# Due times of all engines' steps taken from one table, and the last output block copied and sent in two halves

## The chip, the cores and the metric

The kernel runs on one core of one Trainium2 chip. The metric is the device time of one execution in microseconds; of several executions the median counts. The core's engines each work through a queue of their own, in order: TensorE (PE: matmuls, with weight loads PEld beside them), VectorE (DVE), ScalarE (ACT), GpSimd (POOL) and SyncE (SP, which here only issues DMAs). An instruction that waits holds up all that stands behind it in its queue.

## The reference

Attention with a window of 128 positions and a bias by distance, then a feed-forward layer with a squared ReLU, all in float32:

```python
scores = scale * np.matmul(q, k.transpose(0, 1, 3, 2)) + bias          # 8 batches, 8 heads, 576 positions, 64 wide
scores = np.where((rel >= 0) & (rel < 128), scores, -1e9)
attn = softmax(scores)
x = (attn @ v).transpose(0, 2, 1, 3).reshape(4608, 512)
h = np.maximum(x @ w_in, 0.0)                                           # 512 x 2048
out = h * h @ w_out                                                     # 2048 x 512
```

## The kernel before

The 4608 tokens are cut into nine **chunks** `c` of 512. Attention goes by **couples** `q` (chunk and pair of heads, four to a chunk), each of two **segments** `k = 2q + s` of 256 positions. The float32 matmuls of the feed-forward layer are made of three products of rounded high and low parts (`hh`, `hl`; `w` likewise). The first layer of chunks 0 and 1 is plain (`gemm1`, L224); from chunk 2 on it is done by a scheme of seven products of half size (`M1` to `M7`, L319, in the PSUM tiles `chain` and `rest`), whose weight sums are computed once, during chunk 1, by DVE, ACT and POOL (`weight_sums`), written to DRAM (`ws`) and streamed back for each use (`flow`, L288). A step `n` of this part handles two of the 16 blocks of a hidden layer. The second layer's blocks (`("g", f, m)`, L376) fill the PSUM tiles `acc`; when a chunk is full, `give` copies each of the four blocks to an `o` tile (L382, even blocks on DVE, odd ones on ACT) and `send` writes it out (L386). There are four `o` tiles; some `weight_sums` and pieces of attention use them as well.

Once in two steps `n`, a **visit** `q` (class `Visit`) puts attention work on PE: `one` and `two` multiply the values with the masked weights of couple q-1 (L719), and between them `scores` makes the scores of couple q (L732). What lies between the scores of a couple and the next visit is a long chain over the other engines, for each segment:

- `base` (ACT, L613 and L620) and `fold` (DVE, L632 and L636) move the scores to an SBUF tile `t`;
- `t` (DVE, L400, four) adds the bias and takes the maximum, `e` (ACT, L407, four) the exponentials, `sum` (DVE, L414 and L415) the reciprocal;
- `norm` (POOL, L419) multiplies, `square` (DVE, L471) transposes in squares of 32;
- `write` (SP, L475, four DMAs to the DRAM tile `way`) and `read` (SP, L480) finish the transpose;
- `before` and `same` (POOL, L484) mask the two halves, after which the next visit's `one` can run.

Beside this chain run the drains of the seven products (`s1`, `R`, `s2`, `C21` on ACT; `C11`, `C22`, `C12` on DVE, L324, of which M3 needs C11 and M4 needs C22), the squares `sq`, `high` and `hl` of the hidden layer (L346, L351, L353), and the pieces `x` of the last couple's result (L669 and L684 to L704).

The order of all queues is set in Python when the program is built. `Plan.add` takes each step's engine, its planned length, what it follows, and a **due** time; `Plan.run` repeatedly takes the engine that can start first, and of that engine's steps that can start at about that time the one that is due first. Planned lengths and dues decide the order only: on the chip each engine waits for what it needs. PE's steps are each tied to the PE step before, so their order doesn't depend on dues. Steps with the same due and time are taken in the order of a Python set, which can differ from build to build: rows of an order below are those of one build each. `start` plans the beginning with dues of its own, `middle` all from the second chunk's first layer on.

Of the kernel before, what the change touches and what calls it, by code (L numbers as in the profile page):

```python
# [24 lines left out]
NCH = B * S // 512  # L25
# [6 lines left out]
WAIT = 0.1  # L32
HAND = {"SP": 2.0, "PE": 0.25}
PORT = ('t', 'c', 'h1')
# [29 lines left out]
class Kern:  # L64
# [315 lines left out]
    def give(self, c, m):  # L380
        o = self.out[c, m] = self.op.tile([128, 512], F32, name="o")
        (self.nc.scalar.copy if m % 2 else self.nc.vector.tensor_copy)(o, self.full.pop((c, m)))  # L382

    def send(self, c, m):
        out = self.outd[m * 128 : m * 128 + 128, 512 * c : 512 * c + 512]
        (self.nc.scalar if c == NCH - 1 and m == 3 else self.nc.sync).dma_start(out, self.out.pop((c, m)))  # L386
# [428 lines left out]
class Plan:  # L815


    def __init__(self, wait=WAIT, port=PORT):
        self.steps, self.count, self.wait, self.port = {}, {}, wait, port
# [12 lines left out]
    def run(self):  # L832
# [7 lines left out]
        while near:  # L840
# [16 lines left out]
            same = [r for r in ready if self.steps[r[2]][0] == on and r[0] <= first[0] + max(0.1, self.wait * span)]  # L857
# [132 lines left out]
ACT, DVE, POOL = "Activation", "DVE", "Pool"  # L990
SOFT = dict(M1=0.72, g=0.7, first=2.79, one=0.85, scores=0.75, two=0.65)
# [9 lines left out]
def middle(K, waiting):  # L1001
    P = Plan(0.7, ("t", "ws"))
# [15 lines left out]
    def second(count):  # L1018
        for _ in range(count):
# [6 lines left out]
            if e == NF - 1:  # L1026
                P.add(("give", c, m), ACT if m % 2 else DVE, 0.6, (("g", f, m),), t + 1.5, do(K.give, c, m), "o")
                P.add(("send", c, m), "SP", 0.8, (("give", c, m),), t + 8, do(K.send, c, m), None, "o", 1)

    def chain(q, s, V):  # L1030
        G, k = waiting[q].both[s], 2 * q + s
        n = lambda a, *m: (a, k, *m)
        for m in range(4):
            P.add(n("t", m), DVE, 0.22, (n("t", m - 1) if m else n("fold"),), V + 1.8 + 1.4 * s, do(G.top, m))
            P.add(n("e", m), ACT, 0.4, (n("t", m),) + ((n("e", m - 1),) if m else ()), V + 2 + 1.5 * s, do(G.exp, m))
        P.add(n("sum"), DVE, 0.42, (n("e", 3),), V + 2.4 + 1.4 * s, G.sums)
        P.add(n("norm"), POOL, 1.15, (n("sum"),), V + 2.4 + 1.4 * s, G.norm)
        turned(q, s, V + 2.5 + 1.4 * s, (n("norm"),))
# [11 lines left out]
    def visit(q):  # L1050
# [8 lines left out]
        if new and q + 1 < 4 * NCH:  # L1059
            for a, us in (("qk", 1.4), ("v", 0.9)):  # L1060
                fn = K.load_v if a == "v" else lambda c, p: (K.load_qk(c, p, 0), K.load_qk(c, p, 1))
                P.add((a, q + 1), "SP", us, ((a, q),) if (a, q) in P.steps else (), base + 12 if a == "qk" else base + 14, do(fn, *divmod(q + 1, 4)), a)
# [9 lines left out]
        if G.p < 2:  # L1072
# [3 lines left out]
            dues, reads, room = [16, 16.5, 16, 16.5, 18, 19], (0, 1, 2, 3), {0: ("o", None)}  # L1076
# [203 lines left out]
```

## Time and profile before

| what | value |
|---|---|
| median of 3 runs | 917.92 us (917.68 to 919.81) |
| the profiled execution | 919.04 us |
| its span, first to last instruction | 917.3 us |
| granted TensorE clock | 1.00 throughout |
| instructions | 23301 |
| moved by DMA | 212.96 MB, 232 GB/s on average |

The page gives for each engine the time that it was busy and its share of the span; a row of a timeline has the start (us from the span's start), the length, the engine, the line, the operation with its tiles (out<-in) and a count where equal instructions follow each other; idle time of the engine just before, and what ended it, stands in brackets. SPq and ACTq are rows of DMAs being issued by SP and ACT. In a row of a group, the numbers behind the bar are busy time, the mean of one in ns, and idle time before it. In a row of DMA issues they are the KB of each and the median time from issue to landing. An engine's row in the list of waits has the total, the count and the longest wait.

### The profile page before, as it was taken

How to read it: one execution, taken by the hardware profiler on the slowest of the kernel's cores; microseconds unless marked ns; L12 is line 12 of the kernel's file. 1: busy time of each engine (PE TensorE's matmuls, PEld its weight loads, DVE VectorE, ACT ScalarE, POOL GpSimd, SP SyncE). 2: the span in 40 equal slices, each digit the busy share in tenths (PEclk: the TensorE clock that was granted, in tenths of full speed). 3: DMA queues.
4: the chain of work that ended last, by engine and by line, in shares of the span. 5: the costliest groups of instructions: out<-in, count | busy, mean ns of one | idle time of the engine just before them, and what ended most of it. 6: DMA issues, size and time to landing. Idle time of an engine off the chain costs nothing.

```text
span 917.3 us, 23301 instructions
## 1 busy us (share of the span) xinstructions
PE 905.9 (99%) x8500; PEld 803.1 (88%) x8500; DVE 584.1 (64%) x1595; ACT 466.8 (51%) x1321; POOL 275.8 (30%) x339
## 2 busy tenths in 40 slices
PE   9999999999999999999999999999999999999998
PEld 5688888888889999999999999999999989989997
DVE  6999862776766666565756666667666565554333
ACT  7898663566555545444544544445444454433222
POOL 4213324665732223223322332233223232230000
PEclk9999999999999999999999999999999999999999
DMA  9985328668788888777877778777877776666541
GB/s 343 404 309 170 87 61 265 192 204 282 255 274 278 303 276 276 245 231 228 267 248 246 228 234 278 233 239 234 277 230 238 229 251 197 199 208 216 175 127 46
DMA packets 137425, 212.96 MB, mean 232 GB/s; under 512 B 15200, under 2 KB 49120, under 8 KB 137312
## 3 DMA queue, kind: packets, MB, share of 16 engines
q1 hardware_dynamic: 136880, 210.82, 71.5%
q8 instruction: 68, 1.11, 0.5%
q10 hardware_dynamic: 432, 0.66, 0.3%
q14 instruction: 45, 0.37, 0.1%
HBM read 170.52 MB, written 40.89 MB: 230 GB/s over the span
## 4 chain that ended last, share of the span: by engine, by line
PE 87%; DMA 7%; DVE 2%; ACT 1%; issue 1%; SPq 1%; POOL 1%; POOLq 0%; DVEq 0%; ACTq 0%
PE acc L376 41%; PE chain L319 16%; PE rest L319 12%; PE g L224 8%; PE s L719 4%; PE g L732 2%; DMA raw<-in_dram 2%; DMA qk<-in_dram 1%; PE s L732 1%; DMA ws<-both 1%; DMA flow<-ws 1%; PE at L496 1%; DMA way<-pp 1%; DMA wide<-in_dram 1%; POOL pp L484 1%
## 5 line engine op out<-in xcount | busy, mean ns | idle before, releaser
L376 PE MATMUL acc<-hh,w 128*128 128x512 f32 x1152 | 405.1, 397 | 0.0
L376 PEld LDWEIGHTS acc<-hh,w 128*128 128x128 f32 x1152 | 225.6, 196 | 38.5 <-issue 5.3
L376 PE MATMUL acc<-hl,w 128*128 128x512 f32 x576 | 226.3, 393 | 0.0
L484 POOL TENSOR_SCALAR_AFFINE_SELECT pp<-pp 128x512 f32<-128x512 f32 x128 | 101.8, 796 | 204.5 <-DMA pp<-way 73.9
L324 DVE TENSOR_TENSOR four<-four,rest 128x256 f32<-128x256 f32 x112 | 47.2, 422 | 178.1 <-PE rest L319 176.8
L419 POOL TENSOR_TENSOR t<-t,nm 128x512 f32<-128x512 f32 x64 | 73.3, 1147 | 280.5 <-DVE nm L415 241.1
L319 PEld LDWEIGHTS rest<-xu,flow 128*128 128x128 f32 x1008 | 146.3, 196 | 12.7 <-DVE four L324 0.5
L319 PE MATMUL chain<-tees,flow 128*128 128x256 f32 x1008 | 148.3, 283 | 0.3 <-POOL tees L669 0.3
L319 PE MATMUL rest<-xu,flow 128*128 128x256 f32 x1008 | 148.4, 284 | 0.0
L319 PEld LDWEIGHTS chain<-tees,flow 128*128 128x128 f32 x1008 | 133.1, 197 | 0.9 <-POOL tees L669 0.5
L339 ACT COPY four<-chain 128x256 f32<-128x256 f32 x56 | 20.9, 373 | 221.2 <-PE chain L319 221.2
L376 PEld LDWEIGHTS acc<-hl,w 128*128 128x128 f32 x576 | 112.6, 195 | 12.7 <-DVE hl L353 0.2
L407 ACT ACTIVATE t<-t,nm 128x128 f32<-128x128 f32 x256 | 101.1, 399 | 26.5 <-DVE nm L400 26.3
L224 PE MATMUL g<-xu,w 128*128 128x512 f32 x384 | 95.2, 397 | 0.7 <-ACT r L233 0.7
L224 PEld LDWEIGHTS g<-xu,w 128*128 128x128 f32 x384 | 76.3, 209 | 13.8 <-ACT r L233 1.2
L400 DVE CUSTOM_DVE_ANT_0 t<-t,cst 128x128 f32<-128x128 f32 x256 | 68.5, 314 | 1.2
L632 DVE COPY_PREDICATED t<-cst,s 64x256 f32<-64x256 int32 x100 | 44.6, 446 | 32.6 <-PE s L719 22.4
L471 DVE STREAM_TRANSPOSE pp<-t 128x512 f32<-128x512 f32 x64 | 45.4, 710 | 18.8 <-POOL t L419 18.0
L719 PE MATMUL s<-pp,v 64*64 64x128 f32 (+1 forms) x1792 | 52.7, 248 | 3.3 <-POOL pp L484 2.9
L319 PEld LDWEIGHTS chain<-xu,flow 128*128 128x128 f32 x336 | 48.7, 196 | 4.2
L319 PE MATMUL chain<-xu,flow 128*128 128x256 f32 x336 | 49.4, 284 | 0.0
L407 ACT ACTIVATION_READ_ACCUMULATOR t<-t,nm 128x1 f32 x256 | 49.0, 191 | 0.0
(104 smaller groups left out, 1129.6 us busy)
## 6 DMA issues: line engine op xcount, KB each, us to landing
flow<-ws SPq DMA_DIRECT2D x392, 256.0 KB, 4.0
raw<-in_dram SPq DMA_DIRECT2D x32, 512.0 KB, 8.7
way<-pp SPq DMA_DIRECT2D x256, 64.0 KB, 2.0
pp<-way SPq DMA_DIRECT2D x64, 256.0 KB, 3.6
qk<-in_dram SPq DMA_DIRECT2D x32, 320.0 KB, 4.5
v<-in_dram SPq DMA_DIRECT2D x32, 320.0 KB, 3.5
qk<-in_dram SPq DMA_DIRECT2D x38, 256.0 KB, 4.8
out_dram<-o SPq DMA_DIRECT2D x35, 256.0 KB, 3.1
```

The source lines that it names most:

```text
L224: nc.tensor.matmul(g, w, xs[cc][:, part], start=i == 0, stop=i == 11)
L319: self.nc.tensor.matmul(to, w, x, start=start and k == 0, stop=k == 5, skip_group_check=True)
L324: add = lambda to, x: nc.vector.tensor_tensor(to, to, x, op=ALU.add)
L376: self.nc.tensor.matmul(self.acc[m], w, h, start=(f == 0 and i == 0), stop=(f == NF - 1 and i == 2))
L400: self.nc.vector.tensor_tensor_reduce(self.t[:, m], self.t[:, m], self.K.nrel(2 * self.p + m // 2), -0.125, BIG, ALU.add, ALU.min, self.nm ...
L407: return self.nc.scalar.activation(self.t[:, m], self.t[:, m], AF.Exp, bias=nm[:, 4 + m : 5 + m], scale=-1.0, accum_out=nm[:, m : m + 1],)
L419: self.nc.gpsimd.tensor_tensor(*(x.rearrange("p (j i) c -> p j i c", j=2) for x in (self.t, self.t)), self.rec.unsqueeze(3).to_broadcast([ ...
L471: nc.vector.transpose(squares.rearrange("p b m c -> p m b c"), self.t.rearrange("p m (b c) -> p m b c", c=32))
L484: nc.gpsimd.affine_select(to, self.own, pattern=[[-32 * sign, 4], [0, 4], [-sign, 32]], compare_op=op, fill=0.0, base=0, channel_multiplie ...
L632: nc.vector.copy_predicated(d, mask.unsqueeze(1).to_broadcast([64, 2, 2, 64]), e)
L719: yield self.nc.tensor.matmul(to, w, x, start=first and n < 2, stop=not first, skip_group_check=True)
L732: made = self.nc.tensor.matmul(to, w, x, start=not extra, stop=True, skip_group_check=True)
```

## The change

`LAG` and `DUE` are new tables that take the place of the dues that stood in the code, for every family of steps in `middle`: the chain of attention, the drains' followers, output copies and sends, loads, weight sums, streams. `V` is the planned end of a visit, `t` and `now` the planned end of a PE step. Some dues now lie far before or after the time at which a step can run, so that they act as ranks. `Plan` gets a flag `mixed`: where the first step that can start is one that shares a port in the plan (POOL's, and DVE's `t` and `ws`), the choice is among such steps of both engines. The window in which a later step may be taken first goes from 0.7 to 0.4 of a step's length. The last output block (chunk 8, block 3) is copied half by ACT and half by DVE, and sent in two halves by ACT and SP.

```diff
     def give(self, c, m):
         o = self.out[c, m] = self.op.tile([128, 512], F32, name="o")
+        if (c, m) == (NCH - 1, 3):
+            x = self.full.pop((c, m))
+            self.nc.scalar.copy(o[:, 0:256], x[:, 0:256])
+            self.nc.vector.tensor_copy(o[:, 256:512], x[:, 256:512])
+            return
         (self.nc.scalar.copy if m % 2 else self.nc.vector.tensor_copy)(o, self.full.pop((c, m)))
 
     def send(self, c, m):
         out = self.outd[m * 128 : m * 128 + 128, 512 * c : 512 * c + 512]
-        (self.nc.scalar if c == NCH - 1 and m == 3 else self.nc.sync).dma_start(out, self.out.pop((c, m)))
+        o = self.out.pop((c, m))
+        if (c, m) == (NCH - 1, 3):
+            self.nc.scalar.dma_start(out[:, 0:256], o[:, 0:256])
+            self.nc.sync.dma_start(out[:, 256:512], o[:, 256:512])
+            return
+        self.nc.sync.dma_start(out, o)
...
-            same = [r for r in ready if self.steps[r[2]][0] == on and r[0] <= first[0] + max(0.1, self.wait * span)]
+            alike = lambda name: self.steps[name][0] == on or self.mixed and self.shares(first[2]) and self.shares(name)
+            same = [r for r in ready if alike(r[2]) and r[0] <= first[0] + max(0.1, self.wait * span)]
...
+DUE = {
+    "wait": (0.4, 1), "give": (41.7, 32.5, 45.4, 45.4), "send": (43.2,), "load": (4.4, 9.8), "fill": (45.2, -26.7),
...
-    P = Plan(0.7, ("t", "ws"))
+    P = Plan(DUE["wait"][0], ("t", "ws"), DUE["wait"][1])
...
-            P.add(n("t", m), DVE, 0.22, (n("t", m - 1) if m else n("fold"),), V + 1.8 + 1.4 * s, do(G.top, m))
+            P.add(n("t", m), DVE, 0.22, (n("t", m - 1) if m else n("fold"),), V + DUE["t"][s], do(G.top, m))
```

What this does to the queues shows in three places. With the lines added to `give` and `send`, numbers behind them are ten higher in the changed kernel (L386 is L396, L400 is L410, L471 is L481, L475 is L485, L480 is L490).

**SP ahead of visit 13.** The rows run from the first write (`way<-pp`) of couple 12 to its second read (`pp<-way`); `flow` are streamed weight sums, `out_dram` the sends of chunk 1, `ws` writes of weight sums. Before:

```order
L475 DMA way<-pp 32x4x128 x4
L288 DMA flow_6_1686<-ws_109 128x512
L288 DMA flow_0_1673<-ws_110 128x512
L480 DMA pp<-way 128x512
L288 DMA flow_1_1674<-ws_110 128x512
L386 DMA out_dram<-o 128x512 x2
L475 DMA way<-pp 32x4x128 x4
L386 DMA out_dram<-o 128x512 x2
L480 DMA pp<-way 128x512
```

Now, from the stream ahead of the writes on:

```order
L288 DMA flow_4_1677<-ws_110 128x512
L485 DMA way<-pp 32x4x128 x8
L490 DMA pp<-way 128x512
L284 DMA ws_114<-both_2391 128x512
L490 DMA pp<-way 128x512
L284 DMA ws_114<-both_2391 128x512 x3
```

Both segments' writes now stand together, ahead of both reads, with one write of weight sums between the reads; the four sends have moved behind two more steps of streams.

**DVE ahead of visit 33**, in step n = 56. L400 with its maximum is a `t` of couple 32's second segment, the L324 rows are C11, C22 and C12, L414 and L415 a `sum`, L382 an output copy of chunk 6, L471 (L481) the `square`, `ISA` the instructions of L400 (L410). Before, from a `t` to the second square:

```order
L400 ISA nm 128x1
L324 TENSOR_TENSOR four_1687<-four_1687,rest 128x256
L324 TENSOR_TENSOR four_1688<-four_1688,chain 128x256
L400 ISA t,nm<-t,cst 128x128
L400 ISA nm 128x1
L353 TENSOR_TENSOR hl<-spare,hh 128x512
L324 TENSOR_TENSOR four_1687<-four_1687,rest 128x256
L414 TENSOR_SCALAR nm<-nm 128x3x2
L415 RECIPROCAL nm<-nm 128x2x2
L346 SCALAR_TENSOR_TENSOR r<-four_1687 128x512
L382 COPY o<-acc 128x512
L471 STREAM_TRANSPOSE pp<-t 128x4x4x32
```

Now, from the end of the last `t` on:

```order
L410 ISA nm 128x1
L424 TENSOR_SCALAR nm<-nm 128x3x2
L425 RECIPROCAL nm<-nm 128x2x2
L679 TENSOR_TENSOR o<-o,s 128x256
L679 TENSOR_TENSOR xu<-s,xu 128x256
L424 TENSOR_SCALAR nm<-nm 128x3x2
L425 RECIPROCAL nm<-nm 128x2x2
L481 STREAM_TRANSPOSE pp<-t 128x4x4x32
L324 TENSOR_TENSOR four_1687<-four_1687,rest 128x256
L481 STREAM_TRANSPOSE pp<-t 128x4x4x32
L324 TENSOR_TENSOR four_1688<-four_1688,chain 128x256
L324 TENSOR_TENSOR four_1687<-four_1687,rest 128x256
```

All eight `t` and both sums have moved ahead of C11, and both squares ahead of C12. How C11, C22 and the squares stand to each other differs by visit: in the visits 17 to 19, 21 to 23, 25 to 27 and 29 to 31 both squares stand directly ahead of C11, where the second one stood behind C22 before. Ahead of visit 13 it is C11, C22 and then both squares. In most visits the `hl` of the step before (L353, second) has moved ahead of the folds.

**SP at the start of `middle`**, around the sends of chunk 0. `qk` and `v` are loads of keys, queries and values of later couples; `ws_108<-o` is the copy of an `o` tile that `weight_sums` filled. Before:

```order
L475 DMA way<-pp 32x4x128 x8
L480 DMA pp<-way 128x512 x2
L258 DMA ws_108<-o 128x512
L386 DMA out_dram<-o 128x512 x2
L258 DMA ws_108<-w_250 128x512 x2
L170 DMA qk<-in_dram 128x640
```

Now:

```order
L490 DMA pp<-way 128x512
L170 DMA qk<-in_dram 128x640
L170 DMA qk<-in_dram 128x512
L490 DMA pp<-way 128x512
L175 DMA v<-in_dram 128x640
L170 DMA qk<-in_dram 128x640
L170 DMA qk<-in_dram 128x512
L396 DMA out_dram<-o 128x512
L258 DMA ws_109<-w_292 128x512
L258 DMA ws_108<-o 128x512
L258 DMA ws_108<-w_250 128x512 x2
```

Two couples' keys and one's values have moved ahead of the first send and of that copy. The output copies of blocks 2 and 3 of chunk 0 are the fifth and sixth users of the four `o` tiles; in the changed program the first of them waits for a DMA out of a tile, the other for POOL and a DMA.

More of the change, by code (lines that the diff above doesn't have):

```diff
@@ L990 @@
 ACT, DVE, POOL = "Activation", "DVE", "Pool"
+LAG = {"a0": 6.5, "r0": 3, "s2": 1.5, "h0": 1.5, "l0": 0.5, "w0": 0.5}
+DUE = {
+    "wait": (0.4, 1), "give": (41.7, 32.5, 45.4, 45.4), "send": (43.2,), "load": (4.4, 9.8), "fill": (45.2, -26.7),
+    "base": (-0.7, -16.2), "fold": (-0.3, -21.4), "t": (-71.3, -85.5), "e": (-38, 3.5), "sum": (-31.2, -14.7),
+    "norm": (-33.7, -13.5), "square": (-5.5, -3.6), "first": (-800, -11.2, 10.8, -31.4),
+    "ws": (-14.6, 6.7, -2.7, 31.8, 26.2, 25.3, 29.3, 73.4), "flow": (35.1, 33.2), "sq": (-12.7, 34.4),
+    "high": (-11.2, -14.3), "hl": (-14.3, -2.2), "early": (40.9, 16.3, 33.8, 53.7, 7.9, 22.8),
+    "third": (74.8, 68.8, 53.8, 52, 54.4, 50.8, 73.6, 80.8, 46.8, 54.8, 59.5, 61.6),
+    "last": (-1.9, -17, -18.3, 18, -19.2, -31.5, -13.2, 11, -9.1, 0.3, -27.1, -17.4),
+}
 SOFT = dict(M1=0.72, g=0.7, first=2.79, one=0.85, scores=0.75, two=0.65)
@@ L1033, in chain @@
         for m in range(4):
-            P.add(n("t", m), DVE, 0.22, (n("t", m - 1) if m else n("fold"),), V + 1.8 + 1.4 * s, do(G.top, m))
[L1035 to L1038, printed above, removed]
+            P.add(n("t", m), DVE, 0.22, (n("t", m - 1) if m else n("fold"),), V + DUE["t"][s], do(G.top, m))
+            P.add(n("e", m), ACT, 0.4, (n("t", m),) + ((n("e", m - 1),) if m else ()), V + DUE["e"][s], do(G.exp, m))
+        P.add(n("sum"), DVE, 0.42, (n("e", 3),), V + DUE["sum"][s], G.sums)
+        P.add(n("norm"), POOL, 1.15, (n("sum"),), V + DUE["norm"][s], G.norm)
+        turned(q, s, V + DUE["square"][s], (n("norm"),))
     def turned(q, s, d, after):
@@ L1075, in visit @@
             )
[L1076 removed]
+            dues, reads, room = DUE["early"], (0, 1, 2, 3), {0: ("o", None)}
         else:
@@ L1093, in visit @@
                 prior = prior if prior[0] in P.steps else ()
[L1094 removed]
+                P.add(n("fill", s), POOL if late else "free", 0.4 * late, prior, base + DUE["fill"][s], do(new.fill, s), "t")
                 P.add(
[L1096 removed]
+                    n("base", s), ACT, 1.2 if late else 0.58, (n("scores"), n("fill", s)) + behind("base"), V + DUE["base"][s],
                     do(new.base, s, False), None, ("one", "two") if s else None,
                 )
[L1099 removed]
+                P.add(n("fold", s), DVE, 1.15 if late else 0.9, (n("base", s),) + behind("fold"), V + DUE["fold"][s], do(new.fold, s))
             chain(q, 0, V)
@@ L1115, in middle @@
                 (name, n), engine, us, ((("first", n),), (("relu", n),), (("sq", n),), (("high", n),))[i],
-                t + (-800, 2.5, 3.2, 4)[i], step, (("r", "hh"), None, None, None)[i], (("one", "two"), None, None, "r")[i],
+                t + DUE["first"][i], step, (("r", "hh"), None, None, None)[i], (("one", "two"), None, None, "r")[i],
             )
```

30 lines of the change are left out of this document (13 added, 17 removed).

## The prediction

> **What bounds the kernel now.** I read the page first: which engine fills the span.
>
> ```profile
> PE 905.9 (99%) x8500; PEld 803.1 (88%) x8500; DVE 584.1 (64%) x1595; ACT 466.8 (51%) x1321; POOL 275.8 (30%) x339
> ```
>
> TensorE is busy for 905.9 of 917.3 us, and the change leaves its instructions and their order in `middle` as they are (each PE step is tied to the one before it). So only time in which PE stands still can be won, and a new order can only add such time elsewhere. Second view: who PE waits for (us in total, times, longest).
>
> ```profile
> PE s L719 <- POOL pp L484: 2.9, 2, 2.1
> ```
>
> It sits where a "visit" begins: the first L719 matmuls read tiles that POOL's affine selects (L484) have just masked. Third view: the timeline of PE, rows of L719 that begin a visit (start, length).
>
> ```profile
> 232.59 0.90 PE L719 MATMUL s<-pp,v 64*64 64x64 f32 x32
> 258.48 0.33 PE L719 MATMUL s<-pp,v 64*64 64x64 f32 x2
> ...
> 285.00 0.90 PE L719 MATMUL s<-pp,v 64*64 64x64 f32 x32
> 309.13 0.90 PE L719 MATMUL s<-pp,v 64*64 64x64 f32 x32
> ...
> 695.64 0.79 PE L719 MATMUL s<-pp,v 64*64 64x64 f32 x28
> 719.85 0.90 PE L719 MATMUL s<-pp,v 64*64 64x64 f32 x32
> 744.41 0.33 PE L719 MATMUL s<-pp,v 64*64 64x64 f32 x2
> 769.80 0.90 PE L719 MATMUL s<-pp,v 64*64 64x64 f32 x32
> ```
>
> Between two visits PE always does the same work, so distances tell what is lost better than idle rows do. Undisturbed it is 24.13 (285.00 to 309.13). From visit 12 (232.59) to 13 it is 25.89, from 13 to 14 it is 26.52: 1.76 + 2.39 = **4.15 us lost**. Late in the kernel the pace is 24.21 (695.64 to 719.85); then 24.56 and 25.39: 0.35 + 1.18 = **1.53 us lost** around visit 33. Together 5.68 us can be won in the middle, and something at the tail. No other visit is off pace.
>
> **Visit 13 (terms: -4.15, and what is left).** The chain ahead of it, from the timelines of POOL, DVE and SP:
>
> ```profile
> 241.30 0.90 DVE L632 COPY_PREDICATED t<-cst,s 64x256 f32<-64x256 int32 x2
> 245.21 1.14 DVE L400 CUSTOM_DVE_ANT_0 t<-t,cst 128x128 f32<-128x128 f32 x1
> 247.83 1.05 POOL L419 TENSOR_TENSOR t<-t,nm 128x512 f32<-128x512 f32 x1 [1.62 <-DVE nm L415]
> 249.34 0.70 DVE L471 STREAM_TRANSPOSE pp<-t 128x512 f32<-128x512 f32 x1
> 250.56 1.88 SPq L475 DMA_DIRECT2D way<-pp  x4
> 252.48 0.94 SPq L386 DMA_DIRECT2D out_dram<-o  x2
> 255.51 0.33 SPq L480 DMA_DIRECT2D pp<-way  x1
> 258.98 1.84 POOL L484 TENSOR_SCALAR_AFFINE_SELECT pp<-pp 128x512 f32<-128x512 f32 x2 [2.18 <-PE chain L319]
> ```
>
> The last segment's fold ends at 242.20, but its four L400 stand on DVE among drains, pieces and the other segment's transpose, so that its norm (L419) starts only at 247.83. The transpose then ends at 250.04, the write is issued by 252.44, the read back goes out at 255.51 (3.07 after the write, with two output sends between), and the masks start 3.47 after that. The costs of one, from the page:
>
> ```profile
> L484 POOL TENSOR_SCALAR_AFFINE_SELECT pp<-pp 128x512 f32<-128x512 f32 x128 | 101.8, 796 | 204.5 <-DMA pp<-way 73.9
> ...
> L407 ACT ACTIVATE t<-t,nm 128x128 f32<-128x128 f32 x256 | 101.1, 399 | 26.5 <-DVE nm L400 26.3
> L400 DVE CUSTOM_DVE_ANT_0 t<-t,cst 128x128 f32<-128x128 f32 x256 | 68.5, 314 | 1.2
> ```
>
> In the new order all eight L400 stand directly behind the folds, both sums before the drains, and the transposes behind the first two drains; SP issues both writes, then both reads, and the sends behind them. Step by step from a fold that ends no later than 242.2: four L400 (0.31 each at most) to 243.4; four exponentials, about 0.4 each, on ACT behind a drain, to some 244.6; sums 0.35, to 245.0; norm 1.05 and a handover, to 246.2; transpose 0.70, to about 247.1 instead of 250.04. SP issues the first four writes from about 246, the second four behind them (1.88 each time) by 249.7. With the landing as before (3.07) the read goes out at 252.8, masks start at 256.2 and, at 0.80 each by the mean or 1.84 for the two as here, end at 257.8 to 258.1. PE comes to the visit 1.76 earlier than before, at 256.72, if what it loses between visits 12 and 13 goes as well. So 1.0 to 1.4 us of waiting would be left; with the landing at 2.0, the median of these small writes (row at the tail, below), 0 to 0.3. The sends that stood behind the write are gone, but the loads of weights aren't; I take the middle, **0.6 left (bounds 0 and 1.4)**.
>
> The 1.76 ahead of it are pieces that reach PE late, the largest shown here:
>
> ```profile
> 245.12 0.39 PE L319 MATMUL chain<-tees,flow 128*128 128x256 f32 x1 [0.30 <-POOL tees L669]
> ```
>
> In the new order these pieces (L669, L704) stand ahead of the norms on POOL and of the exponentials on ACT, some 4 us earlier. What comes later instead is the drain L324 behind both sums, which M3 waits for: it would end about 0.15 us before M3 begins. I leave **0.2 (0 to 0.8)** there, and another **0.2 (0 to 1)** half a visit on, where the output copies of chunk 1 now stand between squares and `hl` on DVE, ahead of the block of L376 that needs that `hl`.
>
> **Visit 33 (term: -1.53).**
>
> ```profile
> 732.02 0.41 DVE L324 TENSOR_TENSOR four<-four,chain 128x256 f32<-128x256 f32 x1
> 735.47 0.71 DVE L471 STREAM_TRANSPOSE pp<-t 128x512 f32<-128x512 f32 x1 [0.17 <-DMA flow<-ws]
> 736.22 1.76 SPq L475 DMA_DIRECT2D way<-pp  x4
> 739.57 0.33 SPq L480 DMA_DIRECT2D pp<-way  x1
> 743.47 2.06 POOL L484 TENSOR_SCALAR_AFFINE_SELECT pp<-pp 128x512 f32<-128x512 f32 x2 [3.79 <-DMA pp<-way]
> ```
>
> The same chain. In the new order the second transpose has only C11, the first transpose and C22 ahead of it, not C12, a square and an output copy; C22, the L324 row here, ended at 732.43; with the first transpose done while it waits for its matmul, the second ends near 733.2 instead of 736.18. Everything behind moves by 3.0: masks end at 742.5 instead of 745.53. PE arrives at 744.41 - 0.35 = 744.06. The wait goes with 1.5 us to spare, so half of the shift is nearly enough: **0 left**.
>
> **The visits between.** They keep pace already, so a quicker chain gains nothing; what it could lose is the second rival. 0.
>
> **The start.** `start` and its dues aren't changed: 0. But the first sends of `middle` are. SP now issues key and value loads between the reads and the first send, and the copy of an `o` tile into `ws` comes behind that send. Both free `o` tiles, of which there are four, for the output copies of blocks 2 and 3 of chunk 0.
>
> ```profile
> 143.19 1.53 SPq L480 DMA_DIRECT2D pp<-way  x2
> 147.78 1.69 SPq L170 DMA_DIRECT2D qk<-in_dram  x2
> out_dram<-o SPq DMA_DIRECT2D x4, 256.0 KB, 4.2
> ws<-o SPq DMA_DIRECT2D x2, 256.0 KB, 4.4
> 153.12 0.39 PE L376 MATMUL acc<-hh,w 128*128 128x512 f32 x1
> ```
>
> From a read at 143.2, two pairs of key loads (1.69 each), a second read and a value load (under 0.5 each) bring the send to about 148.1, and two more issues the `ws` copy to 149.0. They land 4.2 and 4.4 us later (this stretch, 143 to 156), at 152.3 and 153.4. The copies take 0.6 to 0.7 and PE wants block 2 at 153.12, block 3 some 0.7 later. That is even, or late by 0.2: **0.3 left (0 to 1.5)**. Before, these copies waited for nothing.
>
> **The tail.**
>
> ```profile
> 913.62 0.59 ACT L382 COPY o<-acc 128x512 f32<-128x512 f32 x1 [0.81 <-PE acc L376]
> L339 ACT COPY four<-chain 128x256 f32<-128x256 f32 x56 | 20.9, 373 | 221.2 <-PE chain L319 221.2
> out_dram<-o ACTq DMA_DIRECT2D x1, 256.0 KB, 2.1
> way<-pp SPq DMA_DIRECT2D x256, 64.0 KB, 2.0
> ```
>
> A copy of half the width saves 0.2 of 0.59 (a drain of 128x256 takes 0.37 on ACT). SP and DVE are free by then, so the halves run side by side. The landing took 2.1 us for 256 KB and 2.0 for 64 KB: half the size saves 0 to 0.1. **-0.25 (0 to -0.5).** [...]
>
> **Sum.** -5.68 + 0.6 + 0.2 + 0.2 + 0 + 0.3 - 0.25 = -4.63. The profiled execution took 919.04 (its span 917.3 and 1.7 around it), which gives 914.4; it lay 1.1 above the median of the runs, 917.92, and within them. Against the median: **913.3 us**. All bounds at their best: 911.7. All at their worst (1.4, 0.8, 1, 1.5 left and no tail): 916.9.
>
> **Rivals.**
>
> *New waits take most of it back.* The queues in visits 12 to 13 and near 153 us are close, and landings there can be longer than medians. With two or three leftovers at their worst, 2.5 to 4.5 are left: 914.7 to 917. For it: the margins of 0.1 to 0.5 above. Against: they lie in four places that don't wait for each other.
>
> *Slower: transposes ahead of C11.* In twelve of the visits between, both transposes now stand on DVE directly ahead of C11, which M3 needs. Visit 25:
>
> ```profile
> 561.18 0.88 PE L319 MATMUL chain<-tees,flow 128*128 128x256 f32 x6
> 561.36 1.05 POOL L419 TENSOR_TENSOR t<-t,nm 128x512 f32<-128x512 f32 x1 [3.01 <-DVE nm L415]
> 562.59 0.88 PE L319 MATMUL rest<-xu,flow 128*128 128x256 f32 x6
> L324 DVE TENSOR_TENSOR four<-four,rest 128x256 f32<-128x256 f32 x112 | 47.2, 422 | 178.1 <-PE rest L319 176.8
> ```
>
> C11's own matmul is done when M7 begins, at 561.18, and M3 begins at 562.59; with C11 (0.42), the transpose (0.71) and a handover ahead, the second norm must end by about 561.3. Before, it ended at 562.41. I work out 560.2 for it now (second sum 2 us earlier, behind exponentials that follow without a drain's wait). If it didn't move, each visit would lose 1.1: 13 us, 926. From 0.62 lost per visit on (norm end past 561.9) the gain and 2.75 more are eaten; at 0.8, 9.6 lost against 4.6 won gives 923. Against it: nothing is left ahead of the second sum but four L400 and two short instructions. What could do it is DVE being held up by POOL: the L400 of 1.14 us above, against a mean of 0.31, began beside a POOL addition. [...]
>
> *The order isn't what holds visit 13.* If landings under load set it (4.4 as near 153 us, not 3.07), the 2.39 stay in place of 0.6, and with the other leftovers as taken 3.1 are left: 915.1, or up to 917 with one of them at its worst.
>
> **Chances.** Forecast (911.7 to 914.7) 0.71; new waits 0.19, a quarter of it still below 915.17; slower 0.04; landings 0.06, counted as within. 0.3% of 917.92 is 2.75 us, about what a measurement of this kernel can tell from no change: faster is below 915.17, slower above 920.67. Faster 0.76, within 0.20, slower 0.04. The range runs from 911.7 to 916.5, which leaves out the slower case, part of the last and the worst of the new waits.
>
> **What would show it.** Distances of L719 starts: 12 to 13 near 24.5, 13 to 14 near 24.7, 32 to 33 and 33 to 34 at 24.2. Sends behind both reads on SP. PE's waits on L484 below 1 us in all. Wrong, if L376 waits for `o` near 153 us by more than 1.5, if the visits from 14 to 32 are further apart than before, or if visit 13 still waits 2 us.

## The result, and the profile after

| | median of 12 | range | granted clock |
|---|---|---|---|
| before, run beside it | 919.34 us | 916.69 to 922.11 | 1.000 in the first profile |
| after | 923.11 us | 921.43 to 928.42 | 0.996 to 1.000 |

The ratio is 1.0049, 95% interval 1.0031 to 1.0067: **slower by half a per cent**, where the prediction said 913.3 and gave 0.04 to slower. The profiled execution after took 924.34 us, its span 922.6, so 5.3 more than the span before.

Who PE waits for, after (us in all, times, longest):

```profile
PE s L729 <- POOL pp L494: 4.0, 3, 3.4
PE acc L376 <- DVE o L387: 0.9, 1, 0.9
PE rest L319 <- DVE xu L679: 0.8, 1, 0.8
PE acc L376 <- ACT o L387: 0.2, 1, 0.2
```

The wait for the masks (L494, before L484) is still there, longer than before, and two waits for output copies are new. The timeline of PE, the rows of L729 (before L719) that begin visits 12 to 15 and 32 to 34, tells where:

```profile
235.49 0.32 PE L729 MATMUL s<-pp,v 64*64 64x64 f32 x2
239.17 1.13 PE L729 MATMUL s<-pp,v 64*64 64x64 f32 x23 [3.36 <-POOL pp L494]
...
266.61 0.90 PE L729 MATMUL s<-pp,v 64*64 64x64 f32 x32
290.77 0.90 PE L729 MATMUL s<-pp,v 64*64 64x64 f32 x32
314.90 0.90 PE L729 MATMUL s<-pp,v 64*64 64x64 f32 x32
...
726.64 0.90 PE L729 MATMUL s<-pp,v 64*64 64x64 f32 x32
750.87 0.90 PE L729 MATMUL s<-pp,v 64*64 64x64 f32 x32
775.09 0.90 PE L729 MATMUL s<-pp,v 64*64 64x64 f32 x32
```

Visit 13 no longer waits (266.61 to 290.77 is 24.16, before 26.52), nor does visit 33 (24.23 and 24.22, before 24.56 and 25.39). But visit 12, which kept pace before, now waits 3.36 us. Its 64 matmuls of L729 and those of the scores between them took 8.07 us from the first to the last; without a wait a visit takes 2.79. So 5.3 were lost, and only 3.4 of them are the wait. The rest is in the granted clock (stretches of the trace: length, then busy time and instructions of each engine, the clock, the DMAs' share and GB/s):

```profile
237.00:239.20 2.20, 0.03 (x4) 0.03 (x4) 0.99 (x1) 0.50 (x1) 1.86 (x3) 1.00 0.47 180
239.20:242.60 3.40, 3.40 (x89) 3.40 (x93) 0.00 (x0) 0.00 (x0) 3.31 (x4) 0.50 0.72 229
242.60:246.00 3.40, 3.40 (x52) 2.69 (x45) 1.78 (x5) 2.64 (x9) 1.00 (x3) 1.00 1.00 372
```

For 3.4 us behind the wait PE runs at half its clock, and 3.4 us at 0.50 lose 1.7. The spread of the twelve times goes with it in part: 3.4 us of 922.6 at half clock make a mean clock of 0.998 for the whole execution, twice as much makes 0.996. The one execution at 1.000 took 921.43; the eight at 0.998 took 921.95 to 924.34; the three at 0.996 took 923.85 to 928.42. That is a range of 7, of which two such stretches are 3.4.

Starts of visits in both traces give the whole account, after minus before (from visit 9 to 12, where the first layer is plain, the pace is 24.4 to 25.1):

| from, to | change, us |
|---|---|
| start of the span to visit 9 (158.05, now 160.19) | +2.14 |
| visit 9 to the start of visit 12 (visit 10 loses 0.7) | +0.76 |
| visit 12 itself (3.23, now 8.07) | +4.84 |
| rest of the way to visit 13 (22.66, now 23.05) | +0.39 |
| visit 13 to 14 | -2.36 |
| visit 14 to 32 (visits 17 and 25 lose 0.4 and 0.5) | +1.02 |
| visit 32 to 34 | -1.50 |
| visit 34 to the end | 0.0 |

The sum is +5.3, the difference of the spans.

Visit 13 doesn't wait, but by little: its last mask ends at 266.27, 0.34 before PE comes, and PE comes 1.7 later than it could, since the way from the end of visit 12 takes 23.05 where an undisturbed one takes 21.3 (24.13 less a visit of 2.8). On pace PE would have waited 1.4 there.

**Why visit 12 waits** stands in SP's queue. Its rows before, the writes of couple 11:

```profile
217.68 1.75 SPq L475 DMA_DIRECT2D way<-pp  x4
...
220.92 1.77 SPq L475 DMA_DIRECT2D way<-pp  x4
```

And after, with the reads behind them:

```profile
212.17 3.75 SPq L284 DMA_DIRECT2D ws<-both  x4
216.01 0.39 SPq L175 DMA_DIRECT2D v<-in_dram  x1
220.52 1.27 SPq L288 DMA_DIRECT2D flow<-ws  x3
221.83 0.43 SPq L258 DMA_DIRECT2D ws<-w  x1
222.31 0.91 SPq L170 DMA_DIRECT2D qk<-in_dram  x2
223.26 1.60 SPq L258 DMA_DIRECT2D ws<-w  x3
224.95 6.43 SPq L485 DMA_DIRECT2D way<-pp  x8
231.56 0.34 SPq L490 DMA_DIRECT2D pp<-way  x1
...
232.86 0.32 SPq L490 DMA_DIRECT2D pp<-way  x1
```

SP issues nothing from 216.40 to 220.52: the next flow copies read what the four weight copies (L284) write, and wait for the last to land, as the chain of waits has it:

```profile
214.66 5.84 DMA ws<-both
```

The queue then goes on with nine large DMAs, of step 16's flow, weight sums 6 and 7 and the keys of couple 14, issued in 4.3 us. Only then come the writes, 10.5 us ahead of the visit where they went out 14.9 ahead before. The first transpose had ended at 221.27 (the timeline of DVE), so its write lay 3.7 in the queue; before, it left 0.03 behind its transpose. And behind these nine the eight writes took 6.43 to issue, 0.8 each on average, where four took 1.75, 0.44 each, so that the reads follow them late as well.

**The start.** The timeline around the output copies of blocks 2 and 3 of chunk 0:

```profile
147.73 0.43 SPq L396 DMA_DIRECT2D out_dram<-o  x1
148.73 0.72 SPq L258 DMA_DIRECT2D ws<-o  x1
153.89 0.69 DVE L387 COPY o<-acc 128x512 f32<-128x512 f32 x1 [8.06 <-PE g L224]
154.64 0.51 PE L376 MATMUL acc<-hh,w 128*128 128x512 f32 x1 [0.88 <-DVE o L387]
155.16 0.59 ACT L387 COPY o<-acc 128x512 f32<-128x512 f32 x1 [5.04 <-DMA ws<-o]
155.79 0.51 PE L376 MATMUL acc<-hh,w 128*128 128x512 f32 x1 [0.18 <-ACT o L387]
```

The send and the `ws` copy go out when the prediction said, but land some 6 later instead of 4.2 to 4.4, behind the loads now issued ahead of them. The copies start then, and PE waits. The last 70 matmuls ahead of visit 9 took 18.03 us from the first's start, 16.20 before: 1.83.

**The tail**, the two half copies in the timeline:

```profile
918.91 0.37 ACT L384 COPY o<-acc 128x256 f32<-128x256 f32 x1 [0.82 <-PE acc L376]
...
919.31 0.42 DVE L385 COPY o<-acc 128x256 f32<-128x256 f32 x1 [0.41 <-ACT o L384]
```

DVE's half copy waits for ACT's (the bracket names what released it), so the halves run one behind the other: 3.76 us from PE's last matmul to the end of the span, 3.74 before.

### The profile page after: what moved, and what is told of

It is laid out like the page before. It is cut to its first block, busy times and chain, and to the rows that moved or that the text cites. A ratio compares the mean times of both kernels' runs of the same rounds, so it can differ in the third digit from the quotient of the medians.

```text
span 922.6 us, 23237 instructions
## 1 busy us (share of the span) xinstructions
PE 907.8 (98%) x8496; PEld 804.6 (87%) x8500; DVE 583.1 (63%) x1596; ACT 466.6 (51%) x1321; POOL 267.1 (29%) x339
## 4 chain that ended last, share of the span: by engine, by line
PE 83%; DMA 8%; DVE 3%; ACT 2%; SPq 2%; POOL 1%; issue 1%; POOLq 0%; DVEq 0%; ACTq 0%
PE acc L376 39%; PE chain L319 16%; PE rest L319 12%; PE g L224 6%; PE s L729 5%; PE g L742 2%; DMA raw<-in_dram 2%; DMA pp<-way 1%; PE s L742 1%; SPq L485 1%; DMA ws<-both 1%; DMA way<-pp 1%; POOL pp L494 1%; ACT t L417 1%; DMA ws<-o 1%
## 5 line engine op out<-in xcount | busy, mean ns | idle before, releaser
L324 DVE TENSOR_TENSOR four<-four,rest 128x256 f32<-128x256 f32 x112 | 47.2, 421 | 214.7 <-PE rest L319 214.0
L494 POOL TENSOR_SCALAR_AFFINE_SELECT pp<-pp 128x512 f32<-128x512 f32 x128 | 98.6, 770 | 218.0 <-DMA pp<-way 162.8
L429 POOL TENSOR_TENSOR t<-t,nm 128x512 f32<-128x512 f32 x64 | 69.7, 1091 | 242.3 <-DVE nm L425 180.5
L410 DVE CUSTOM_DVE_ANT_0 t<-t,cst 128x128 f32<-128x128 f32 x256 | 63.6, 305 | 1.8
L729 PE MATMUL s<-pp,v 64*64 64x128 f32 (+1 forms) x1792 | 54.3, 250 | 4.2 <-POOL pp L494 4.0
L242 DVE TENSOR_TENSOR hl<-r,hh 128x512 fp32r<-128x512 f32 x32 | 26.2, 818 | 41.6 <-ACT hh L240 41.5
L729 PEld LDWEIGHTS s<-pp,v 64*64 64x64 f32 x1792 | 42.1, 135 | 9.6 <-POOL pp L494 5.0
```

What stands on the lines that cost most here:

```text
L242: nc.vector.tensor_tensor(hl, r, hh.bitcast(F32), op=ALU.subtract)
L324: add = lambda to, x: nc.vector.tensor_tensor(to, to, x, op=ALU.add)
L410: self.nc.vector.tensor_tensor_reduce(self.t[:, m], self.t[:, m], self.K.nrel(2 * self.p + m // 2), -0.125, BIG, ALU.add, ALU.min, self.nm ...
L429: self.nc.gpsimd.tensor_tensor(*(x.rearrange("p (j i) c -> p j i c", j=2) for x in (self.t, self.t)), self.rec.unsqueeze(3).to_broadcast([ ...
L494: nc.gpsimd.affine_select(to, self.own, pattern=[[-32 * sign, 4], [0, 4], [-sign, 32]], compare_op=op, fill=0.0, base=0, channel_multiplie ...
L729: yield self.nc.tensor.matmul(to, w, x, start=first and n < 2, stop=not first, skip_group_check=True)
```

## The experiments

The plan takes steps of equal due and time in the order of a Python set, which can differ from build to build. To compare orders at all, the experiments e1 to e11 fix it. Beside them ran the kernel before, with medians of 926.95, 926.33, 926.06 and 927.49 in the four sets, where the first comparison had 919.34; e12 makes it likely that this is another build of the same source. The ratios are to it.

### e1 and e2: both kernels with named ties

```diff
-            t, due, name = min(same, key=lambda r: (r[1], r[0]))
+            t, due, name = min(same, key=lambda r: (r[1], r[0], str(r[2])))
```

> The kernel before, with one edit: steps of equal due and equal planned time are taken in the order of their names, where the plan took them in whatever order a Python set gave (so the order of `start`, and of a few steps of `middle`, could differ from one build to the next). It is the base for what follows. Theory (the dues of `middle` decide the result, not these ties): 916.5 to 920.5, within 0.3% of the kernel before; clock 1.000; visits 12 to 13 and 13 to 14 again 1.5 to 2.5 over the pace of 24.13. Rival (ties are worth a per cent): outside 914 to 922.

> The changed kernel with the same edit. Theory: 921 to 925, 4 to 6 over e1; visit 12 waits 3 to 3.6 for the masks, and the granted clock is 0.5 for some 3 us behind that wait, so that the mean clock is 0.998. Rival (the result was a matter of ties): within 2 of e1.

Measured: e1 920.73 (919.49 to 922.01), 0.2 above the expected range, ratio 0.9934 (0.9910 to 0.9958). e2 923.72 (920.63 to 927.56), ratio 0.9968 (0.9949 to 0.9987). So the change costs 3.0 with these ties. In e1 visits 12 to 13 and 13 to 14 are 25.81 and 25.61 apart, as expected. In e2's profile, which is of the fastest of its twelve executions, visit 12 waits 1.8, less than expected, but the clock is at 0.50 behind it all the same and the visit takes 6.22. The same source as before, with other ties, is 0.7% faster than the build beside it: ties matter more than I had allowed for.

### e3: couple 11's writes ahead of everything

```diff
+LATER = {
+    **{x: (("write", 23),) for x in (("flow", 16, 4), ("flow", 16, 5), ("flow", 16, 6), ("qk", 14), ("ws", 6, "a2"), ("ws", 7, "a0"))},
+}
...
+        after = tuple(after) + LATER.get(name, ())
         self.steps[name] = (engine, us, after, due + NUDGE.get(name, 0), do, rooms(take), rooms(free), lag)
```

> e2 with couple 11's two writes put ahead of the loads and copies that stood in front of them on SP: flow copies 4, 5 and 6 of step 16, the key load 14, the last load of weight sum 6 and the loads of weight sum 7 now follow write 23. Theory (SP's queue at visit 12 is what costs): the first write goes out near 221.3 instead of 224.95, both take 1.8 to issue instead of 3.2 each, visit 12 waits less than 0.5, the clock stays at 1.000, and the time is 4.5 to 5.5 below e2: 917 to 919. Rival A (couple 11's transposes come too late, 0.7 and 1.0 later against their visit than before, and the queue adds little): visit 12 still waits 2 or more, time at most 3 below e2. Rival B (the DMA engines are full then in whatever order): the writes still take 6 in all, no gain.

Measured: 932.77 (928.94 to 935.07), ratio 1.0065 (1.0039 to 1.0092): 9 slower than e2, a miss. Visit 12 did go as the theory says: it begins at 236.16, waits for nothing and takes 2.79, and each burst of four writes issues in 1.8, so neither rival holds. The loss is elsewhere: visit 13 stands still for 2.7, for a reason that the profile doesn't name, and comes to 29.30 with half clock behind it (the first 128x512 matmul behind the visit takes 0.73, behind visit 12 0.51). The longest of PE's waits:

```profile
PE chain L319 <- ACT tees L714: 9.5, 1, 9.5
```

The loads of weight sum 7 have a due 73 behind their step; once held back they lost their place to every flow copy, and went out only at 286. Pieces of the attention results wait for the last copy of that sum, and PE waited for those pieces ahead of visit 16. So the edit tested too much at once, and e7 repeats it with less.

### e4: the first sends ahead of the loads

```diff
+    **{x: (("send", 0, 1), ("ws", 0, "a0")) for x in (("qk", 10), ("v", 10), ("ws", 1, "a0"), ("ws", 0, "a1"))},
...
-                P.add(("send", c, m), "SP", 0.8, (("give", c, m),), t + DUE["send"][0], do(K.send, c, m), None, "o", 1)
+                P.add(("send", c, m), "SP", 0.8, (("give", c, m),), t + (DUE["send"][0] if c else 8), do(K.send, c, m), None, "o", 1)
```

> e2 with the first output sends and the first load of weight sum 0 ahead of the loads of keys 10, values 10 and the other weights, and the due of chunk 0's sends as before (8 behind the block). Theory (sends behind these loads land late and the output copies of blocks 2 and 3 of chunk 0 wait for their tiles): PE's waits of 0.88 and 0.18 near 155 go, visit 9 begins 1.1 to 1.6 earlier against the start of `middle`, time 1.1 to 1.6 below e2, with visit 12's wait still there. Rival (those copies wait for something else, or the loads that now come later cost visit 10 as much): within 0.5 of e2.

Measured: 922.98 (918.70 to 927.05), ratio 0.9953 (0.9932 to 0.9975). In the trace the step is as expected: no wait for output copies, and the 70 matmuls ahead of visit 9 take 16.20, where e2 needs 17.47. The first two sends land after 3.1 and 3.3 there and the `ws` copy after 3.5, where it was some 6 behind the loads. The median is only 0.7 below e2's, less than expected, within the spread that the half clock makes in both (mean clocks of 0.994 to 1.000 in e4, 0.995 to 1.000 in e2); visit 12 still waits 1.9.

### e5 and e6: both kernels with a second order of ties

```diff
-            t, due, name = min(same, key=lambda r: (r[1], r[0]))
+            t, due, name = min(same, key=lambda r: (r[1], r[0], crc32(str(r[2]).encode())))
```

> The kernel before with its ties broken in a second fixed order (by a checksum of the step's name): against e1, 110 of 196 DVE positions and 27 of 67 SP positions of `start` hold other steps, and in `middle` 89 of 943 on DVE and 57 of 648 on SP. Theory (the ties alone are worth half a per cent, since two builds of the kernel before gave medians of 919.3 and 926.95): the median differs from e1's 920.7 by 2 us or more, and the trace shows other visits that wait. Rival (builds don't matter, the 926.95 came from something else): within 1.5 of e1.

> The changed kernel with the same second order of ties. `start` is then the one of e5; in `middle` only 11 SP positions differ from e2, none on the other engines. Theory: PE waits at visit 12 again, 1.5 to 3.5, whatever `start` does, so 922 to 926, and the difference to e5 is free of the ties of `start`. Rival (the wait at visit 12 came from one draw of ties): visit 12 begins on pace, 918 to 920.

Measured: e5 922.93 (921.96 to 924.72), ratio 0.9961 (0.9947 to 0.9975); e6 920.99 (918.76 to 923.67), ratio 0.9940 (0.9917 to 0.9963). With these ties **the changed kernel is the faster one**, by 1.9 (the ranges overlap), and 1 below what was expected of it. The timeline of PE and a stretch of the trace in e5, at visit 13:

```profile
263.30 1.55 PE L719 MATMUL s<-pp,v 64*64 64x64 f32 x30 [5.00 <-POOL pp L484]
```

```profile
262.20:269.00 6.80, 5.70 (x124) 5.29 (x125) 0.81 (x2) 1.65 (x6) 0.98 (x2) 0.51 0.98 325
```

The visit that waited 2.07 in the first profile, at full clock, here waits 5.00 and brings 6.8 us of half clock. In e6 visit 12 waits 2.3, with a stretch of half clock (0.50 from 236 to 239), visits 10 and 17 lose 0.7 and 1.4, and no output copy near 155 is waited for: which of the small waits come depends on the ties of `start`; visit 12's came in all three builds of the changed kernel.

### e7: only the loads behind the writes

```diff
+    **{x: (("write", 23),) for x in (("qk", 14), ("ws", 6, "a2"), ("ws", 7, "a0"))},
...
-                    w(name), engine, us, after + before, d, step, "o" if name == "o" else None,
+                    w(name), engine, us, after + before, t if j == 7 and name[0] == "a" else d, step, "o" if name == "o" else None,
```

> e2 with couple 11's writes ahead of the key load 14, the last load of weight sum 6 and the loads of weight sum 7; the flow copies of step 16 stay ahead of them, and the loads of sum 7 keep an early due, which they lost in e3 (their chain came 30 us late there and PE waited 9.5 for it). Theory (what stands between SP's blocked stretch and the writes costs visit 12): first write near 220.5, visit 12 waits under 0.5, no stretch of half clock, visit 16 on pace, time 2 to 4 below e2's 923.7: 920 to 921.7. Rival (the writes are slow because of the bytes queued before them, flow copies above all): the two writes still take 5 to 6 to issue, visit 12 waits 1 or more, within 1.5 of e2.

Measured: 918.98 (916.84 to 920.02), ratio 0.9913 (0.9890 to 0.9937), **4.7 below e2**. SP's row of the writes:

```profile
220.72 5.26 SPq L485 DMA_DIRECT2D way<-pp  x8
```

The first write goes out 14.2 ahead of the visit. The 5.26 are two bursts of 1.8 with the wait for the second transpose between them, so the slow issue is gone too. Visit 12 begins at 234.93, waits for nothing and takes 2.80, and the clock is 1.000. The six DMAs that stood between the flow copies and the writes are what visit 12 waited for. But visit 13, which the changed kernel and e2 reached without a wait, now waits 1.2 (13 to 14 is 25.63).

### e8: the loads, the sends and the tail together

```diff
-            x = self.full.pop((c, m))
+            x, p = self.full.pop((c, m)), self.tp.tile([128, 4, 128], F32, name="t").rearrange("p m c -> p (m c)")
             self.nc.scalar.copy(o[:, 0:256], x[:, 0:256])
-            self.nc.vector.tensor_copy(o[:, 256:512], x[:, 256:512])
+            self.nc.vector.tensor_copy(p[:, 256:512], x[:, 256:512])
...
```

(with the edits of e4 and e7)

> e7 with e4's edit as well (first sends ahead of the loads), and the last block's two half copies into two different tiles, so that neither waits for the other. Theory: the gains add: 0.7 below e7 from the sends, and the time from PE's last matmul to the span's end falls from 3.76 to 3.35, the second copy beginning beside the first and not 0.41 behind it. Time 919 to 921, the fastest so far, at most 0.2% from e1. Rival: the sends' edit moves the loads on and a visit from 9 to 12 waits for them, so nothing adds; or the half copies still run one behind the other, because they read one bank, and the tail stays at 3.76.

Measured: **916.71 (916.07 to 917.36)**, ratio 0.9890 (0.9865 to 0.9915), better than expected: 2.3 below e7 and 4.0 below e1, its range apart from e1's and not from e7's. The rows of PE that begin visits 12, 13 and 14:

```profile
232.83 0.90 PE L731 MATMUL s<-pp,v 64*64 64x64 f32 x32
...
259.21 0.90 PE L731 MATMUL s<-pp,v 64*64 64x64 f32 x32
283.35 0.90 PE L731 MATMUL s<-pp,v 64*64 64x64 f32 x32
```

No visit of the three waits. From 12 to 13 it is still 26.38, 2.25 over the pace. PE's weight loads wait there for two drains above all (L329 on ACT 0.9, L324 on DVE 0.6), for a `base` on ACT (0.6) and for an output copy (0.4). The tail's rows:

```profile
910.83 0.37 ACT L384 COPY o<-acc 128x256 f32<-128x256 f32 x1 [0.82 <-PE acc L376]
...
911.23 0.42 DVE L385 COPY t<-acc 128x256 f32<-128x256 f32 x1 [0.41 <-ACT o L384]
```

Here the rival was right in what happens: with two different target tiles DVE still starts when ACT ends, and the tail is 3.76. What the two have in common is the PSUM tile that they read. In the trace it is a semaphore of ACT's copy that releases DVE's, 0.41 us after DVE came free. What the halves would do without that semaphore wasn't tried, and no run shows whether one bank would hold them apart.

### e9: the new order without SP's part of the table

```diff
-LAG = {"a0": 6.5, "r0": 3, "s2": 1.5, "h0": 1.5, "l0": 0.5, "w0": 0.5}
+LAG = {"a0": 2, "r0": 3, "s2": 1.5, "h0": 1.5, "l0": 1.5, "w0": 2.5}
...
-    "wait": (0.4, 1), "give": (41.7, 32.5, 45.4, 45.4), "send": (43.2,), "load": (4.4, 9.8), "fill": (45.2, -26.7),
+    "wait": (0.4, 1), "give": (41.7, 32.5, 45.4, 45.4), "send": (8,), "load": (12, 14), "fill": (45.2, -26.7),
...
-    "ws": (-14.6, 6.7, -2.7, 31.8, 26.2, 25.3, 29.3, 73.4), "flow": (35.1, 33.2), "sq": (-12.7, 34.4),
+    "ws": (20, 20, 20, 20, 20, 20, 60, 60), "flow": (17, 17), "sq": (-12.7, 34.4),
```

> e2 with the numbers that order SP put back to those of before: the dues of sends (8), loads (12 and 14), weight sums (20 and 60) and flow copies (17), and the lags of the weight sums (2, 1.5, 2.5). The new dues of tops, exponentials, sums, norms, transposes, pieces and drains stay. Theory (the gain at visits 13 and 33 comes from these, the loss at visit 12 from SP's part): first write of couple 11 some 14 us ahead of visit 12, no wait there; 13 to 14 and 32 to 34 at the pace; no wait on output copies near 155; 917 to 919.5, 4 to 6 below e2. Rival (the new order of DVE and POOL is itself what makes visit 12 late): visit 12 waits 1.5 or more, 921 and up. Open: weight sum 4's copies and the flow copies of step 17 come 9 later in this plan; if PE waits for those, near 262, the time is above 919.5 for that reason.

Measured: 917.57 (915.87 to 917.87), ratio 0.9905 (0.9888 to 0.9921), 6.2 below e2 and 3.2 below e1. Visit 12 begins on pace and waits for no mask, 32 to 34 are on pace too, and the 70 matmuls ahead of visit 9 take 16.20. But visit 13 waits for its masks, against what was expected:

```profile
260.44 0.89 PE L729 MATMUL s<-pp,v 64*64 64x64 f32 x29 [1.41 <-POOL pp L494]
```

13 to 14 is 25.83, in e1 25.61, so the new order of DVE, ACT and POOL alone wins nothing there. It brings the second read of couple 12 out 3.1 sooner behind visit 12 than in the first profile, but the read lands after 6.2 instead of 3.3. Of the 3.2 below e1 the visits from 12 on carry 2.0 in the traces (21, 32 and 33 win 2.7, others lose 0.7). The rest lies ahead of visit 9, where the profile of e1, of its slowest execution, is 2.7 behind, 1.5 of it a wait in `start`, whose order is the same in both. Against e2, SP's numbers lose 3.4 at visit 12 and 1.3 near 155, and win 1.7 at visit 13.

### e10: waits of chosen lengths

```diff
+            for _ in range(AGAIN.get(self.k, 1) if sign < 0 else 1):
+                nc.gpsimd.affine_select(
...
+AGAIN = {2 * v - 1: n for v, n in ((19, 5), (22, 8), (24, 9), (26, 11), (28, 11), (30, 11), (32, 12), (34, 14))}
```

(on e8)

> e8 with longer masks ahead of eight visits: the second mask of the second segment is applied 5 to 14 times instead of once (it changes nothing after the first), at visits 19, 22, 24, 26, 28, 30, 32 and 34, so that PE waits there. By 0.76 each and e8's slack at these visits the waits are about 0.7, 1.9, 2.2, 2.9, 3.3, 3.8, 4.7 and 6.8. Theory (a long wait costs more than itself: the granted clock falls to one half for some 3.3 us about 3 us after the wait begins, which takes 1.7 more): the 0.7 wait costs 0.7 and keeps the clock at 1.00, each of 3.3 and more costs itself and 1.5 to 3, and those of 1.9 to 2.9 either, since waits of 1.7 and 2.3 had such a stretch in e2 and e6 and waits of 1.9 and 2.1 had none in e4 and before. Rival (the half clock belongs to what runs near visit 12, not to the wait): every visit costs its wait within 0.3. [...]

Measured once: 965.26, mean clock 0.982. Visit 19 hardly waited; the other waits came out at 1.54, 4.26, 5.11, 4.76, 4.56, 5.85 and 8.32, most of them longer than planned, and none between 1.6 and 4.2. Three of the eight, from the start of the visit that waits to 20 us ahead of the next one (without a wait these stretches would be 4.13 to 4.21 long):

```profile
477.83:483.79 5.96, 4.42 (x131) 3.93 (x131) 4.67 (x8) 3.41 (x9) 1.74 (x2) 1.00 0.34 102
...
693.81:704.32 10.51, 5.95 (x131) 5.46 (x131) 5.32 (x7) 3.12 (x8) 4.56 (x5) 0.84 0.14 33
749.00:761.59 12.59, 6.74 (x135) 6.23 (x135) 4.59 (x6) 3.34 (x8) 5.71 (x7) 0.73 0.11 26
```

At visit 22 the wait of 1.54 kept the clock at 1.00 and the next visit came 25.96 later, 1.83 over the pace. At visit 30 a wait of 4.56 cost 6.30, at visit 32 one of 5.85 cost 8.39. All six waits over 4 cost 1.7 to 2.8 more than themselves and brought half clock, 3.41 us of it twice and 6.83 four times, never another length here (e3, with waits of 2.7 and 9.5, has a mean clock of 0.993, which makes some 13 us in all). The six stretches begin at 531.1, 585.7, 643.7, 698.3, 753.0 and 811.0, so 54.6 or 58.0 apart, 16 or 17 times 3.413. The profile after has the same step: one stretch of 3.413 from 239.18, behind visit 12, and another that begins 682.67 later, at the end of the span, 200 times 3.413. The length of a wait doesn't decide alone: e2's visit 12 went to half clock after 1.8 of waiting, e6's after 2.3, while waits of 1.54 here, 1.9 in e4 and 2.07 before did not.

Below 4 it goes, as far as these traces show it, with where the wait falls on a grid of that step. The profiles before and after, cut into windows of 3.413 (before, from a stretch that begins at 918.76, behind the last instruction), have 535 windows at full clock that were followed by full clock, with PE busy for 0.49 or more of each, and three that were followed by half clock, with PE busy for at most 0.13; two of the three are at the end of the program. Ahead of e10's six stretches PE was busy for at most 0.40 of the window, ahead of the one of e2's visit 12, the first row here, for 0.48. The rows behind it are the two windows over which the first profile's wait of 2.07 was spread:

```profile
234.35:237.76 3.41, 1.65 (x68) 1.40 (x71) 1.25 (x1) 1.84 (x3) 2.64 (x4) 1.00 0.44 157
```

```profile
256.57:259.98 3.41, 2.23 (x17) 1.89 (x15) 2.05 (x3) 0.99 (x2) 1.16 (x3) 1.00 0.89 279
259.98:263.40 3.42, 2.53 (x122) 2.53 (x122) 1.97 (x3) 0.32 (x2) 0.84 (x1) 1.00 1.04 365
```

### e11: e8 with the second order of ties

> e8 with the second order of ties. Theory (with visit 12 and the sends mended no visit near its limit is left, so that the draw of ties matters little): 915.5 to 918, visit 12 on pace. Rival (each draw finds another place): 919 or more, with a visit other than 12 that waits over 1.

Measured: 918.28 (916.63 to 919.43), ratio 0.9908 (0.9892 to 0.9924). Visit 12 is on pace, but visit 13 waits 2.0 and takes 6.77 in all in the profiled execution, the slowest of the five, whose mean clock of 0.998 makes some 3.7 us at half clock; the other four have 1.000. So the rival holds in part: the draw still moves a wait, though by two draws (1.6 apart) less than in the kernel before.

### e12: the kernel before, built once more

> The kernel before once more, unchanged; beside the experiments its median was 926, beside the changed kernel 919.3. Theory (another build drew other ties): the order of DVE's and SP's rows differs from the first profile's, the time is either near 919 or near 926, and if near 926 a visit of 12 to 14 waits 4 or more with one or two stretches of half clock of 3.4 behind it, as e5's visit 13 did (wait 5.0, 7.7 lost in all). Rival (the order is the same in all builds and the later runs were disturbed in some other way): rows in the same order as in the first profile, and the extra 7 spread over all visits.

Measured: 923.91 (923.09 to 925.31), against 927.49 for the build beside it, same source: ratio 0.9969 (0.9945 to 0.9994). That is between the two times expected. DVE's and ACT's rows stand in another order than in the first profile, and visit 13 begins its masked work late:

```profile
263.63 1.55 PE L719 MATMUL s<-pp,v 64*64 64x64 f32 x30 [4.06 <-POOL pp L484]
```

So one source gives a visit 13 that waits 1.1 (e1), 2.07 (the first profile), 4.06 or 5.00 (e5). The trace of the build at 926 to 927 was not taken; that it is a still worse draw of the same kind is an inference.

### The draws side by side

| kernel | medians by draw of ties | visits 12 to 14 (at pace 48.3) |
|---|---|---|
| before | 919.3, 920.7, 922.9, 923.9, about 926.5 | 52.4, 51.4, 58.0, 55.3, no trace |
| after | 921.0, 923.1, 923.7 | 54.6, 55.3, 53.6 |
| e8 and e11 | 916.7, 918.3 | 50.5, 54.5 |

The mean over the draws is 922.7 before and 922.6 after; five and three draws are too few to tell the two apart. The measured 1.0049 stands for these two programs; as a statement on the table of dues it compares one draw of after with the best seen of before.

## Why the prediction was wrong

- **That visit 33 would be mended: right**, by the mechanism that was worked out. 32 to 34 came to the pace, and the masks end 1.65 before PE comes (749.22 against 750.87; said: 1.5).
- **That visit 13 would be mended: right in the number, in part by luck.** 13 to 14 came to 24.16 (said: 24.7), with the sends behind both reads on SP. But PE came 1.7 late, by the loss that the prediction took as won; on pace it would have waited 1.4, the top of the range that was worked out. In e7, e9 and e11, where visit 12 keeps pace, visit 13 waits 1.2, 1.4 and 2.0; in e8 it doesn't.
- **"No other visit is off pace ... The visits between ... 0": this is the step that failed.** It took a visit that keeps pace before to keep it after. What was put at 0 measured 6.6: 4.8 in visit 12, 0.8 from visit 9 to 12, 1.0 from 14 to 32. I walked SP's queue for visits 13 and 33 and for the first sends, but not for visits 9 to 12, where the same table puts weight copies, flow copies, a key load and weight loads ahead of couple 11's writes. Visit 12 had 2.1 to spare (masks end at 230.47, visit at 232.59) and its first write lost 4.4. The visit took 8.07 instead of 2.79; e7 takes that away by moving six DMAs, e9 by SP's old numbers.
- **The cost of a wait** was taken as its length. Visit 12's 3.36 cost 1.9 more, and longer waits up to 2.8 more (e10), by the half clock. The first profile hid this, since its longest wait, 2.07, passed at full clock.
- **The 1.76 ahead of visit 13 (said: 0.2 left)** didn't come: 22.66 became 23.05, with the longest of the waits now for a piece on DVE (`xu`, 0.8) behind the `t` and `sum` steps that had been moved forward. The step looked at the pieces that were late before, not at what the new order makes late; e8 loses 2.25 there, to drains above all.
- **The start (said: 0.3, bounds 0 to 1.5):** the mechanism was right, the size was off. The term is the landing, taken as 4.2 and 4.4 and measured near 6 behind the moved loads; 1.83 was lost. e4 and e8 take it away.
- **The tail (said: -0.25):** 0.0, since the halves don't run side by side. e8 shows that the shared target tile isn't the reason; DVE's copy waits for a semaphore of ACT's. (What was taken for the landing rests on two rows alone, 2.1 for 256 KB on ACT and 2.0 for 64 KB on SP.)
- **Rivals.** "New waits take most of it back" named the right kind of loss at the right places but for visit 12, and so stopped at 917. "Slower: transposes ahead of C11" didn't happen: in the profile after, PE waits for C11 nowhere. "The order isn't what holds visit 13" isn't refuted: the 2.39 went in the changed kernel, but in e9, where the transposes are earlier too but the second read lands after 6.2, 1.4 of waiting comes back.
- **What the numbers are against.** The prediction measured from a median of one build. Five draws of the same source span 919.3 to 926.5, so a gain of 4.6 read from one trace was no larger than the luck of that trace. The kernel's text said that ties can fall differently; no range was made from it.

## What to carry to other kernels

Where a change reorders a whole queue, walk that queue for every wait that has little to spare, the ones that keep pace most of all: ask how many bytes (here some 2.4 MB) now stand between a short, urgent DMA and the engine that waits for it. Count a PE wait of several microseconds with the clock that it costs afterwards (here 1.7 to 2.8 more for waits of 3.36 to 8.32); of those of about two some cost it here and some didn't. And where the build breaks ties by chance, fix the ties first: here the same source varied by more than the change did.

## What the runs showed of the hardware

- After PE has stood still the granted clock falls to 0.50, for 3.41 or 6.83 us in the profile after and in e10. Every wait over 3.3 had half clock with it: 3.36 after, 4.06 in e12, 5.00 in e5, 9.5 in e3 and the six of 4.26 to 8.32 in e10. Of shorter ones 1.8 (e2), 2.0 (e11), 2.3 (e6) and 2.7 (e3) had it; 1.54 (e10), 1.6 and 1.9 (e4) and 2.07 (before) had not.
- The stretches begin 16 or 17 times 3.413 us apart in e10, 200 times that after. At full clock, half clock followed windows of that grid with PE busy for 0.13 or less (after, and at the end of before), at most 0.40 (e10) and 0.48 (e2); full clock followed the 535 others before and after, from 0.49 up.
- 64 KB writes that took 0.44 us each to issue on SP before (four in 1.75) took 0.8 after (eight in 6.43), with some 2.4 MB of DMAs issued in the 4.4 us ahead of them (nine DMAs of 256 to 320 KB). In e8, with three flow copies ahead of them and not the other six, eight took 4.10, the wait for the second transpose among them.
- A 256 KB send landed after 6.0 us behind five loads of 256 to 320 KB (after), after 3.1 ahead of them (e4).
